# An expert loop's down projection: token rows straight out of the product, in place of a transposed result that is turned back

## The chip, the core and the metric

The kernel runs on one core of one Trainium2 chip. The metric is the device time of one execution in microseconds (us), lower is better. The core's engines work side by side, each through its own queue in order: TensorE (PE; its weight loads are listed apart as PEld), VectorE (DVE), ScalarE (ACT), GpSimd (POOL) and SyncE (SP), which here only starts transfers.

## The reference

An attention step gives 49,152 rows `x` of 128 numbers (4 batches of 12,288). Each row then goes through a mixture of 8 experts with one expert per row, and only if its skip score is positive:

```python
out = x.copy()
xc = x[x @ w_skip > 0]
probs = softmax(xc @ w_gate); e_idx = argmax; gate_w = probs of that expert
for e in range(8):
    h = np.maximum(xc[e_idx == e] @ w1[e], 0)          # 128 -> 1024
    y[e_idx == e] = gate_w[:, None] * (h @ w2[e])      # 1024 -> 128
out[x @ w_skip > 0] = xc + y
```

The change touches the last product, `h @ w2[e]`, and what follows it.

## The kernel before

**First part.** Attention runs in tiles of 128 queries. Each finished row is written to the output and, with its gate, its index and a scale, to a scratch table `scr` in which the rows of an expert lie together.

**Expert loop.** The second part works through groups of 2,048 rows of one expert, four blocks `s` of 512 tokens each. The first group is interleaved with the end of the attention (`peel`); the others run in a hardware loop whose body is the four blocks and whose count, 17 here, is read from a table at run time. A block is held transposed, channels on the partitions: `up` makes 8 chunks of 128 hidden channels x 512 tokens, `down` adds all chunks up to a result of 128 output channels x 512 tokens in one PSUM bank.

**Three products for one.** Weights and activations are split into two halves of 16 bits, `hi` and `lo`; each chunk costs the products hi·hi, lo·hi and hi·lo. So a block has 24 products in `up` and 24 in `down`, all of 512 columns. Each chunk of `up` fills one of four PSUM banks (pool `ps_h`); ACT takes `h_hi` out (relu, L294), then DVE takes `h_lo` out (L295), and only then is the bank free for the chunk four later.

**What follows `down` before the change.** ACT copies the bank to `yT` with the weights' scale `y_sc` (L310). In the next block, after the fourth chunk of `up`, `finish` has TensorE turn `yT` back in four transposes of 128 tokens (L315, bank pool `ps_x`); DVE works out the row indices (`ids`, L322) and adds gate times result to the input row (`o`, L326, one for each 128 tokens); POOL scatters the rows in four indirect transfers (L184). Then SP loads the next rows (`load_x`).

**Order.** The order on each engine is the order of the calls (`tc.manual_schedule()`); each engine runs its list in order and waits where it needs another's result. Besides the blocks' own work the loop prepares the next expert's weights: `split_w2` in block 0 (ACT makes `w2_hi`, L261, then DVE `w2_lo`, L263), `w_scale` spread over blocks 1 and 2 (DVE finds the largest weights, L207 to L216; a small TensorE product, L219, spreads them over the partitions; DVE reads it, L222, and makes the scales, L224 to L229), `split_w1` in block 3. `previous_stage_wait` marks where an engine makes sure of its block before; the loop's stages let no engine run two blocks ahead of another.

Of the kernel before, what the change touches and what calls it, by code (L numbers as in the profile page):

```python
# [9 lines left out]
F32 = mybir.dt.float32  # L10
# [5 lines left out]
ALU = mybir.AluOpType  # L16
AX = mybir.AxisListType
PSUM = bass.MemoryType.PSUM
# [6 lines left out]
def kernel(  # L25
# [11 lines left out]
    nc = tc.nc  # L37
# [117 lines left out]
    w2_hi = wp.tile([P, FC, C], F16, name="w2_hi")  # L155
    w2_lo = wp.tile([P, FC, C], F16, name="w2_lo")
    yTs = [wp.tile([P, ST], F32, name=f"yT{s}") for s in range(2)]
    xin = [wp.tile([P, TT, ROW], F32, name=f"xin{s}") for s in range(NST)]
    x16s = [wp.tile([P, 2, TT, C], F16, name=f"x16{i}") for i in range(2)]
    xT = [wp.tile([P, 2 * TT, P], F16, name=f"xT{s}") for s in range(NST)]  # L160
# [2 lines left out]
    def alloc_h(pool):  # L163
        h.update(hi=pool.tile([P, FC, ST], F16, name="h_hi"), lo=pool.tile([P, FC, ST], F16, name="h_lo"))
# [133 lines left out]
    def down(s):  # L298
# [10 lines left out]
                yield  # L309
        nc.scalar.activation(out=yTs[s % 2], in_=ps, func=AF.Copy, scale=y_sc[:, 0:1])  # L310

    def finish(s, g=None):
        ps = alloc["x"]()
        for t in range(TT):
            nc.tensor.transpose(ps[:, t * P:(t + 1) * P], yTs[s % 2][:, t * P:(t + 1) * P], ident)  # L315
        ids = xin[s].bitcast(I32)[:, :, C + 1:C + 2]
        own = op.tile([P, TT, 1], I32, name="ids")
        if g is None:
            nc.vector.tensor_copy(own, ids)
        else:  # L320

            nc.vector.scalar_tensor_tensor(out=own, in0=place[:, s, :].unsqueeze(2), scalar=low[:, bass.ds(g, 1)], in1=ids,  # L322
                                           op0=ALU.add, op1=ALU.max)
        o = op.tile([P, TT, C], F32, name="o")
        for t in range(TT):
            nc.vector.scalar_tensor_tensor(out=o[:, t, :], in0=ps[:, t * P:(t + 1) * P],  # L326
                                           scalar=xin[s][:, t, C:C + 1], in1=xin[s][:, t, 0:C],
                                           op0=ALU.mult, op1=ALU.add)

        def write():  # L330
            for t in range(TT):
                scatter_rows(out, own[:, t, :], o[:, t, :], NT - 1, "out")

        if g is None and not ready:
            held.append(write)
        else:
            write()

    def make_table():
        en = accs["run"]  # L340
# [48 lines left out]
    def peel(load_next):  # L389
        for s in range(NST):  # L390
            for c in range(FC):
                up(s, [c])
                if s > 0 and c == 3:
                    finish(s - 1)
                    load_next(s - 1)
                if s >= 2 and c == XP2:
                    x_transpose(s - 2)
                yield
            for _ in down(s):
                yield  # L400
            yield

    order = tc.manual_schedule()
    order.__enter__()
    with ExitStack() as p1:
        kprep = p1.enter_context(tc.tile_pool(name="kprep", bufs=1))
        kvm = p1.enter_context(tc.tile_pool(name="kvm", bufs=2))
# [607 lines left out]
        while t < NTILE + LAG - 1 or next_l or jobs:  # L1015
            t += 1
            b, tb = divmod(t, TPB)
            live = t < NTILE
            late_a.extend(next_l)
            next_l.clear()  # L1020
            if 0 <= t - TLAG < NTILE:
                p_transpose(t - TLAG)
            if live:
                scores(t, range(2) if t > 1 else [1])
            if 0 <= t - LAG < NTILE:
                attend(t - LAG)
            if live:
                row_max(t)
            if t in q_late:
                q_late.pop(t)()  # L1030
            if live and pools and next(pools[0], "end") == "end":
                pools.pop(0)
            run_late(early_a)
            run_late(split_a)
            if 0 <= t - 1 < NTILE:
                p_hi(t - 1)
            run_late(late_a)
            if live:
                row_exp(t)
            run_late(early_g)  # L1040
            run_late(split_v)
            run_late(early_v)
            if 0 <= t - 1 < NTILE:
                p_lo(t - 1)
            if live:
                if t % GT == 0:
                    if t > 0 and t // GT + QA < NGRP:
                        load_q(t // GT + QA)
                if b + 1 < B:
                    for k, r in KV_T.get(tb, ()):  # L1050
                        load_kv(b + 1, k, [r])
                if b + 1 < B and tb == PREP_T[0]:
                    work = prep_kv(b + 1)
                    preps += [(t + x - tb, work) for x in PREP_T]
                if t in PAD_T:
                    write_pads(PADS.pop(0))
            if t == NTILE - FIRST:
                assert not PADS and (SNAPR < 0 or first_writes)
                early.append(first_group())
            if early and live and next(early[0], "end") == "end":  # L1060
                early.pop(0)
            if t == NTILE:
                p_s.close()
                p_kv.close()
                p_q.close()
                alloc_h(p1.enter_context(tc.tile_pool(name="hp1", bufs=1)))
                ps_up = p1.enter_context(tc.tile_pool(name="ps_up", bufs=4, space=PSUM))
                alloc["h"] = lambda: ps_up.tile([P, ST], F32, name="up_ps")
            ph = t % GT
            if ph == 1 and t // GT + 2 < NGRP:  # L1070
                q_split(t // GT + 2, t)
            run_jobs(ph)
            if preps and preps[0][0] == t:
                next(preps.pop(0)[1], None)
            if live and b + 1 < B:
                for k, r in KV_T.get(tb - 4, ()):
                    if r == R - 1:
                        pools.append(pool_kv(b + 1, k))
            for _ in range(2 * (t >= NTILE)):
                next(first)  # L1080
# [5 lines left out]
        for _ in first:  # L1086
            pass
        n_it = nc.values_load(cumi[0:1, 0:1], min_val=1, max_val=NG + 1)
        idle = alloc["h"]()
        for _ in range(W4):  # L1090
            nc.tensor.matmul(idle, w1_hi[:, 0:P], h["hi"][:, 0, :], start=True, stop=True)

    with ExitStack() as p2:
        alloc_h(p2.enter_context(tc.tile_pool(name="hp", bufs=1)))
        ps_h = p2.enter_context(tc.tile_pool(name="ps_h", bufs=4, space=PSUM))
        ps_y = p2.enter_context(tc.tile_pool(name="ps_y", bufs=1, space=PSUM))
        ps_x = p2.enter_context(tc.tile_pool(name="ps_x", bufs=2, space=PSUM))

        alloc.update(h=lambda: ps_h.tile([P, ST], F32, name="h_ps"), x=lambda: ps_x.tile([P, ST], F32, name="x_ps"),
                     y=lambda: ps_y.tile([P, ST], F32, name="y_ps"))  # L1100
        alloc["w"] = alloc["x"]
        tc.prologue_barrier()
        order.__exit__(None, None, None)
        with tc.For_i(0, n_it, 1, hint_engines=(mybir.EngineType.PE,), iteration_sync="staggered") as i:
            for s in range(NST):
                prv = (s - 1) % NST
                with tc.manual_schedule():
                    up(s, range(0, 1))
                    for eng in (nc.gpsimd, nc.sync):
                        tc.previous_stage_wait(eng.engine)  # L1110
                    up(s, range(1, 3))
                    for eng in (nc.vector, nc.scalar, nc.tensor):
                        tc.previous_stage_wait(eng.engine)
                    up(s, range(3, 4))
                    if s == 0:
                        split_w2()
                    finish(prv, i if s == 0 else i + 1)
                    if s == 0:
                        load_w(i + 1)
                    load_x(load_start(i if s == 0 else i + 1), prv)  # L1120
                    up(s, range(4, FC))
                    x_transpose((s + 2) % NST)
                    if s == 1:
                        scale = w_scale()
                        next(scale)
                    if s in (1, 2):
                        next(scale, None)
                    if s == NST - 1:
                        split_w1()
                    for _ in down(s):  # L1130
                        pass
                if s < NST - 1:
                    tc.stage_boundary()
        finish(NST - 1, n_it)


_INS = ["q", "kv", "w_sr", "moe_w_skip", "moe_w_gate", "moe_w1", "moe_w2"]
# [35 lines left out]
```

## Time and profile before

| | |
|---|---|
| median of 3 runs | 1768.91 us (1766.88 to 1768.92) |
| the profiled execution, its own time | 1771.09 us |
| span of its trace | 1768.6 us |
| granted TensorE clock, mean of the span | 0.994 |
| loop, from its first product to its last | 1020 to 1759 us |

The trace's times count from the span's start. A line of the time line has start, duration, engine, source line, operation, what is written and read, the shapes and a count of merged instructions (the duration is then of all of them together); in square brackets stands how long the engine was idle before it and what released it. A TensorE product's duration holds the passage through the array, so products overlap: what one costs the engine is the distance between two starts.

### The profile page before, as it was taken

To read this page: it belongs to the slowest core of one execution; us is meant where nothing else is said; L and a number is where in the kernel's file an instruction comes from. 1 tells how busy PE (TensorE), PEld (TensorE's weight loads), DVE (VectorE), ACT (ScalarE), POOL (GpSimd) and SP (SyncE) were. 2 spreads that over 40 slices of the span, in tenths; PEclk is the share of its full clock that TensorE was granted. 3 is DMA by queue.
4 is the path that set the end of the run, shared out by engine and by line. 5 is a ranking of instruction groups with operands and counts; after the bars stand their busy time and mean duration, and the time that the engine had idled before them with its cause. 6 is when DMAs were issued, how large, how long until landed. Compare 5 with 4: busy or idle time off the path is not lost. (4 is left out here: it accounts for less than half of the span.)

```text
span 1768.6 us, 41455 instructions
## 1 busy us (share of the span) xinstructions
PE 1722.5 (97%) x13918; PEld 1242.3 (70%) x13918; DVE 1491.0 (84%) x3181; ACT 1314.3 (74%) x2487; POOL 631.0 (36%) x796
## 2 busy tenths in 40 slices
PE   5999999999999999999999899999999999999997
PEld 4999999999999998999898444444444444444443
DVE  7888899988998898999997778888877888888886
ACT  4888888888888888888897456666666666666664
POOL 3234333444334343323231323333333333333334
PEclk9999999999999999999999999999999999999999
DMA  7999999999999999999997333433333333333333
GB/s 222 213 200 237 230 198 213 225 233 222 211 224 229 222 191 232 205 188 210 218 210 157 98 79 99 102 99 98 99 101 99 97 97 99 103 101 98 100 105 79
DMA packets 608482, 284.81 MB, mean 161 GB/s; under 512 B 495440, under 2 KB 564176, under 8 KB 608336
## 3 DMA queue, kind: packets, MB, share of 16 engines
q1 hardware_dynamic: 586736, 222.76, 62.6%
q0 software_dynamic: 21600, 60.19, 13.1%
q8 instruction: 82, 1.34, 0.3%
q14 instruction: 64, 0.52, 0.1%
HBM read 90.47 MB, written 72.30 MB: 92 GB/s over the span
## 5 line engine op out<-in xcount | busy, mean ns | idle before, releaser
L295 DVE SCALAR_TENSOR_TENSOR h_lo<-h_ps,h_hi 128x512 f16<-128x512 f32 x544 | 343.8, 687 | 140.6 <-ACT h_hi L294 140.3
L184 POOL DMA_INDIRECT out_dram<-o,ids x288 | 283.1, 983 | 484.2 <-DVE o L326 415.4
L663 ACT ACTIVATE p_sb<-s_ps,nm 128x768 f32<-128x768 f32 x384 | 347.1, 904 | 117.0 <-DVE nm L658 113.1
L658 DVE TENSOR_REDUCE nm<-s_ps 128x1 f32<-128x768 f32 x384 | 365.4, 952 | 71.7 <-PE s_ps L652 68.6
L294 ACT ACTIVATE h_hi<-h_ps 128x512 f16<-128x512 f32 x544 | 316.9, 597 | 49.7 <-PE h_ps L293 30.8
L713 PE MATMUL acc_ps<-v_hi,pt 128*128 128x138 f16 x3072 | 320.0, 224 | 2.4 <-DMA pt<-p 2.3
L713 PEld LDWEIGHTS <-pt 128*128 128x128 f16 x4608 | 275.3, 97 | 64.1 <-issue 56.9
L713 PE MATMUL acc_ps<-v_lo,pt 128*128 128x138 f16 x1536 | 293.0, 223 | 0.0
L650 PE MATMUL s_ps<-k_hi,q_hi 128*128 128x384 f32 x768 | 291.8, 380 | 0.4 <-ACT k_hi L505 0.4
L671 DVE SCALAR_TENSOR_TENSOR p<-p_sb,p 128x512 f16<-128x512 f32 x384 | 270.3, 704 | 3.0 <-ACT p L667 1.6
L631 POOL TENSOR_TENSOR q_lo<-q_sb,q_hi 128x256 fp32r<-128x256 f32 (+1 forms) x190 | 146.8, 773 | 334.4 <-DVE p L671 198.4
L652 PE MATMUL s_ps<-k_hi,q_lo 128*128 128x384 f32 x768 | 259.1, 337 | 0.0
L651 PE MATMUL s_ps<-k_lo,q_hi 128*128 128x384 f32 x768 | 258.5, 337 | 0.0
L667 ACT ACTIVATE p<-p_sb 128x512 f16<-128x512 f32 x384 | 243.1, 633 | 5.5 <-DMA pt<-p 2.8
L291 PE MATMUL h_ps<-xT,w_hi 128*128 128x512 f16 x544 | 207.1, 381 | 6.5 <-issue 6.5
L310 ACT ACTIVATE yT<-y_ps,y_sc 128x512 f32<-128x512 f32 x68 | 46.7, 687 | 216.6 <-PE y_ps L307 213.2
L307 PEld LDWEIGHTS <-w_hi 128*128 128x128 f16 x1152 | 112.7, 98 | 134.8 <-issue 1.4
L292 PE MATMUL h_ps<-xT,w_hi 128*128 128x512 f16 x544 | 207.2, 381 | 0.0
L293 PE MATMUL h_ps<-xT,w_lo 128*128 128x512 f16 x544 | 207.2, 381 | 0.0
L307 PE MATMUL y_ps<-h_hi,w_hi 128*128 128x512 f16 x544 | 206.2, 379 | 0.0
L307 PE MATMUL y_ps<-h_hi,w_lo 128*128 128x512 f16 x544 | 206.2, 379 | 0.0
L307 PE MATMUL y_ps<-h_lo,w_hi 128*128 128x512 f16 x544 | 195.1, 379 | 0.0
(215 smaller groups left out, 2927.7 us busy)
## 6 DMA issues: line engine op xcount, KB each, us to landing
q_sb<-in_q_dram SPq DMA_DIRECT2D x96, 256.0 KB
out_dram<-rows SPq DMA_DIRECT2D x96, 256.0 KB
xin<-scr SPq DMA_DIRECT2D x75, 276.0 KB
w_raw<-in_moe_w_dram SPq DMA_DIRECT2D x34, 512.0 KB, 3.5
kvt<-in_kv_dram POOLq DMA_DIRECT2D x54, 256.0 KB
pt<-p SPq DMA_TRANSPOSE x384
kvt<-in_kv_dram SPq DMA_DIRECT2D x11, 512.0 KB
kvt<-in_kv_dram SPq DMA_DIRECT2D x20, 256.0 KB
```

Of the source, the lines that this page charges most:

```text
L184: ins = nc.gpsimd.indirect_dma_start(out=dst, out_offset=bass.IndirectOffsetOnAxis(ap=ids, axis=0), in_=src, in_offset=None, bounds_check= ...
L294: nc.scalar.activation(out=h["hi"][:, c, :], in_=ps, func=AF.Relu)
L295: nc.vector.scalar_tensor_tensor(out=h["lo"][:, c, :], in0=ps, scalar=0.0, in1=h["hi"][:, c, :], op0=ALU.max, op1=ALU.subtract)
L307: nc.tensor.matmul(ps, w[:, c, :], h[x][:, c, :], start=(i == 0), stop=(i == len(terms) - 1))
L650: nc.tensor.matmul(s[:, h, :HK], q_hi, k_hi[:, sl], start=True, stop=False)
L651: nc.tensor.matmul(s[:, h, :HK], q_hi, k_lo[:, sl], start=False, stop=False)
L652: nc.tensor.matmul(s[:, h, :HK], q_lo, k_hi[:, sl], start=False, stop=True)
L658: nc.vector.tensor_reduce(out=NM[t], in_=S_PS[t][:, :, :HK], axis=AX.XY, op=ALU.max, negate=True)
L663: nc.scalar.activation(out=P_SB[t], in_=S_PS.pop(t)[:, :, :HK], func=AF.Exp, bias=NM.pop(t))
L667: nc.scalar.activation(out=P16[t][:, 0, :], in_=p_flat(t)[:, 0:KD * P], func=AF.Copy, scale=2.0 ** PEXP)
L671: LO[:] = [nc.vector.scalar_tensor_tensor(out=p16[:, 1, :], in0=p_flat(t)[:, 0:KD * P], scalar=2.0 ** PEXP, in1=p16[:, 0, :], op0=ALU.mult ...
L713: nc.tensor.matmul(ps[:, j % 2, :], w, v[a][:, k, :], start=(i == 0), stop=(i == len(AVL) - 1))
```

## The change

In the loop, and for the last block of the first group, `down_rows` takes the place of `down`: the hidden values of 128 tokens are the stationary operand and `w2` (128 columns) streams past them, so the result has tokens on the partitions. That makes 96 products of 128 columns in a block, into four PSUM banks, one for each 128 tokens. `yT` and the transposes go; the gates are multiplied with `y_sc` by one small DVE instruction (`gy`), and the rows are taken out of the four banks as the first thing of the next block, ahead of its `up`; the scatter and the loads stay where they were. With four banks for the result, four are left for `up`; the small product of `w_scale` takes one of those too, and its step is moved behind block 2's `down_rows`. The first group's hidden tiles are kept for the loop, and `down_rows` of its last block stands behind the reading of the loop's count.

```diff
+    gy = wp.tile([P, TT, 1], F32, name="gy")
...
+    def down_rows(s):
+        ps = alloc["r"]
+        for c in range(FC + DL):
+            for t in range(TT):
+                sl = slice(t * P, (t + 1) * P)
+                if c < FC:
+                    for w in (w2_hi, w2_lo):
+                        nc.tensor.matmul(ps[t], h["hi"][:, c, sl], w[:, c, :], start=(c == 0 and w is w2_hi), stop=False)
+                if c >= DL:
+                    nc.tensor.matmul(ps[t], h["lo"][:, c - DL, sl], w2_hi[:, c - DL, :], start=False,
+                                     stop=(c == FC + DL - 1))
+
     def finish(s, g=None):
         ps = alloc["x"]()
         for t in range(TT):
             nc.tensor.transpose(ps[:, t * P:(t + 1) * P], yTs[s % 2][:, t * P:(t + 1) * P], ident)
+        send_out(s, [ps[:, t * P:(t + 1) * P] for t in range(TT)], xin[s][:, :, C:C + 1], g)()
+
+    def out_rows(s, g):
+        nc.vector.tensor_scalar(out=gy, in0=xin[s][:, :, C:C + 1], scalar1=y_sc[:, 0:1], scalar2=None, op0=ALU.mult)
+        return send_out(s, alloc["r"], gy, g)
+
+    def send_out(s, ps, gates, g):
...
-            nc.vector.scalar_tensor_tensor(out=o[:, t, :], in0=ps[:, t * P:(t + 1) * P],
-                                           scalar=xin[s][:, t, C:C + 1], in1=xin[s][:, t, 0:C],
-                                           op0=ALU.mult, op1=ALU.add)
+            nc.vector.scalar_tensor_tensor(out=o[:, t, :], in0=ps[t], scalar=gates[:, t, :],
+                                           in1=xin[s][:, t, 0:C], op0=ALU.mult, op1=ALU.add)
...
-            for _ in down(s):
-                yield
+            if s < NST - 1:
+                for _ in down(s):
+                    yield
...
+    with ExitStack() as p2:
+        ps_y = p2.enter_context(tc.tile_pool(name="ps_y", bufs=1, space=PSUM))
+        alloc["r"] = [ps_y.tile([P, ST], F32, name=f"y_ps{t}")[:, 0:C] for t in range(TT)]
+        down_rows(NST - 1)
         idle = alloc["h"]()
...
+        p_up.close()
         ps_h = p2.enter_context(tc.tile_pool(name="ps_h", bufs=4, space=PSUM))
-        ps_y = p2.enter_context(tc.tile_pool(name="ps_y", bufs=1, space=PSUM))
-        ps_x = p2.enter_context(tc.tile_pool(name="ps_x", bufs=2, space=PSUM))
...
+        alloc["h"] = lambda: ps_h.tile([P, ST], F32, name="h_ps")
+        alloc["w"] = alloc["h"]
...
                 with tc.manual_schedule():
+                    write = out_rows(prv, i if s == 0 else i + 1)
                     up(s, range(0, 1))
...
                     up(s, range(3, 4))
                     if s == 0:
                         split_w2()
-                    finish(prv, i if s == 0 else i + 1)
+                    write()
...
-                    if s in (1, 2):
+                    if s == 1:
                         next(scale, None)
                     if s == NST - 1:
                         split_w1()
-                    for _ in down(s):
-                        pass
+                    down_rows(s)
+                    if s == 2:
+                        next(scale, None)
...
-        finish(NST - 1, n_it)
+        out_rows(NST - 1, n_it)()
```

## Rows read from the trace of the kernel before

**Rows 1.** The page: busy time by engine; the costliest DVE group.

```profile
PE 1722.5 (97%) x13918; PEld 1242.3 (70%) x13918; DVE 1491.0 (84%) x3181; ACT 1314.3 (74%) x2487; POOL 631.0 (36%) x796
...
L295 DVE SCALAR_TENSOR_TENSOR h_lo<-h_ps,h_hi 128x512 f16<-128x512 f32 x544 | 343.8, 687 | 140.6 <-ACT h_hi L294 140.3
```

**Rows 2.** Windows: one pass of the loop, busy us (instructions) by engine, clock, DMA.

```profile
1498.91:1542.20 43.29, 43.29 (x210) 20.73 (x209) 35.19 (x82) 27.95 (x54) 15.72 (x16) 1.00 0.39 99
```

**Rows 3.** Time line of TensorE over that pass: where its stages begin.

```profile
1498.91 0.38 PE L291 MATMUL h_ps<-xT,w_hi 128*128 128x512 f16 x1
...
1501.50 0.60 PE L315 MATMUL x_ps<-ident,yT 128*128 128x128 f32 x4
1501.93 0.38 PE L291 MATMUL h_ps<-xT,w_hi 128*128 128x512 f16 x1
...
1504.52 0.38 PE L307 MATMUL y_ps<-h_hi,w_hi 128*128 128x512 f16 x1
...
1509.70 0.38 PE L291 MATMUL h_ps<-xT,w_hi 128*128 128x512 f16 x1
...
1531.41 0.38 PE L291 MATMUL h_ps<-xT,w_hi 128*128 128x512 f16 x1
...
1542.20 0.38 PE L291 MATMUL h_ps<-xT,w_hi 128*128 128x512 f16 x1
```

**Rows 4.** Time line of TensorE in the attention: products of 138 columns.

```profile
600.45 0.22 PE L713 MATMUL acc_ps<-v_lo,pt 128*128 128x138 f16 x1
...
601.35 0.22 PE L713 MATMUL acc_ps<-v_lo,ptq 128*128 128x138 f16 x1
```

**Rows 5.** Time line of TensorE: two products of the routing, 8 and 1 columns.

```profile
986.48 0.17 PE L812 MATMUL acc_ps<-inner,ones_bf 128*128 128x8 bf16 x1
986.51 0.16 PE L813 MATMUL acc_ps<-odd,ones_bf 128*128 128x1 bf16 x1
```

**Rows 6.** Time line of DVE over the same pass of the loop.

```profile
1500.62 2.49 DVE L295 SCALAR_TENSOR_TENSOR h_lo<-h_ps,h_hi 128x512 f16<-128x512 f32 x4 [2.47 <-ACT h_hi L294]
1503.36 1.28 DVE L263 SCALAR_TENSOR_TENSOR w_lo<-w_raw,w_sc,w_hi 128x1024 f16<-128x1024 f32 x1 [0.26 <-ACT w_hi L261]
...
1518.49 2.34 DVE L207 TENSOR_REDUCE w_max<-w_raw 128x1 f32<-128x1024 f32 x2
...
1521.07 0.48 DVE L216 TENSOR_SCALAR w_dg<-ident,w_max 128x128 bf16<-128x128 f32 x2
...
1524.66 0.22 DVE L322 SCALAR_TENSOR_TENSOR ids<-place,low,xin 128x4 int32<-128x4 f32 x1
1524.79 1.12 DVE L326 SCALAR_TENSOR_TENSOR o<-x_ps,xin 128x128 f32<-128x128 f32 x4
1525.82 2.48 DVE L295 SCALAR_TENSOR_TENSOR h_lo<-h_ps,h_hi 128x512 f16<-128x512 f32 x4
...
1529.26 0.42 DVE L222 TENSOR_REDUCE w_max<-x_ps 128x2 f32<-128x256 f32 x1
...
1530.25 0.20 DVE L229 TENSOR_SCALAR y_sc<-w_exp 128x1 f32<-128x1 f32 x1
```

**Rows 7.** Time line of the weight loads: the second of block 0's down projection.

```profile
1504.70 0.10 PEld L307 LDWEIGHTS <-w_lo 128*128 128x128 f16 x1 [0.29 <-DVE w_lo L263]
```

**Rows 8.** Time line where the loop begins.

```profile
1018.08 0.69 ACT L310 ACTIVATE yT<-acc_ps,y_sc 128x512 f32<-128x512 f32 x1 [11.98 <-remote]
...
1020.13 0.58 PE L291 MATMUL h_ps<-xT,w_hi 128*128 128x512 f16 x1 [6.54 <-issue]
```

**Rows 9.** The page: transfers of instructions, count, MB and share.

```profile
q8 instruction: 82, 1.34, 0.3%
```

**Rows 10.** Time line of the end: last products, first rows, first scatter.

```profile
1758.25 0.59 PE L307 MATMUL y_ps<-h_lo,w_hi 128*128 128x512 f16 x2
...
1760.32 0.87 DVE L326 SCALAR_TENSOR_TENSOR o<-x_ps,xin 128x128 f32<-128x128 f32 x3 [0.33 <-PE x_ps L315]
...
1760.94 0.98 POOL L184 DMA_INDIRECT out_dram<-o,ids  x1 [3.31 <-DVE o L326]
```

More of the change, by code (lines that the diff above doesn't have):

```diff
@@ L332, in write @@
                 scatter_rows(out, own[:, t, :], o[:, t, :], NT - 1, "out")
[L334 to L337, printed above, removed]
+        return (lambda: held.append(write)) if g is None and not ready else write
     def make_table():
@@ L404 @@
     order.__enter__()
+    p_up = ctx.enter_context(ExitStack())
     with ExitStack() as p1:
@@ L1065 @@
                 p_q.close()
-                alloc_h(p1.enter_context(tc.tile_pool(name="hp1", bufs=1)))
-                ps_up = p1.enter_context(tc.tile_pool(name="ps_up", bufs=4, space=PSUM))
+                alloc_h(ctx.enter_context(tc.tile_pool(name="hp", bufs=1, side="right")))
+                ps_up = p_up.enter_context(tc.tile_pool(name="ps_up", bufs=4, space=PSUM, side="right"))
                 alloc["h"] = lambda: ps_up.tile([P, ST], F32, name="up_ps")
@@ L1091 @@
             nc.tensor.matmul(idle, w1_hi[:, 0:P], h["hi"][:, 0, :], start=True, stop=True)
-    with ExitStack() as p2:
-        alloc_h(p2.enter_context(tc.tile_pool(name="hp", bufs=1)))
+        p_up.close()
         ps_h = p2.enter_context(tc.tile_pool(name="ps_h", bufs=4, space=PSUM))
-        ps_y = p2.enter_context(tc.tile_pool(name="ps_y", bufs=1, space=PSUM))
-        ps_x = p2.enter_context(tc.tile_pool(name="ps_x", bufs=2, space=PSUM))
-        alloc.update(h=lambda: ps_h.tile([P, ST], F32, name="h_ps"), x=lambda: ps_x.tile([P, ST], F32, name="x_ps"),
-                     y=lambda: ps_y.tile([P, ST], F32, name="y_ps"))
-        alloc["w"] = alloc["x"]
+        alloc["h"] = lambda: ps_h.tile([P, ST], F32, name="h_ps")
+        alloc["w"] = alloc["h"]
         tc.prologue_barrier()
```

## The prediction, made before the changed kernel was run

> **What bounds the kernel now.** I read the page first: TensorE is busy for 97% of the span, DVE for 84% [rows 1]. The change lies in the expert loop, so the windows of one pass of the loop come next: TensorE is busy for all of its 43.29 us at full clock, DVE for 35.19 [rows 2]. Then the time line of TensorE through that pass. Twelve products of 512 columns take 2.59 us (1501.93 to 1504.52), 0.2158 each; a block's 48 take 10.36. The four transposes hold TensorE for 0.43 (1501.50 to 1501.93). Blocks 1 and 2 together last 21.71, which is 0.13 more than two such blocks: the small product of `w_scale`. Four blocks and that are 43.29 [rows 3]: nothing is left over, TensorE never waits in the loop. Anything taken from it is a gain, and any new wait on it is a loss, at once. The page's 544 `h_lo` [rows 1] are 32 for each pass, so there are 17 passes, and 0.1 us in a pass is 1.7 us.
>
> DVE has room, but not everywhere. Before the first `h_lo` of a block it stands idle (2.47 us in block 0), and that first `h_lo` starts 1.71 us after the block's first product (1500.62 against 1498.91) [rows 3, 6]; I use 1.65 for the other blocks, whose ACT work is the same. Four `h_lo` take 2.48 together and one 0.687 [rows 1, 6], so they follow each other every 0.60, a little faster than the chunks (3 x 0.2158 = 0.647).
>
> **TensorE's own work.** No row has 128 columns of 16 bits at full clock, but its neighbours stand on both sides. Fifteen products of 138 columns, each with a weight load of its own as everywhere in this program (as many loads as products [rows 1]), take 0.90 us, 60.0 ns each [rows 4]; 512 columns take 215.8 [rows 3]. The line through both gives 55.8 ns at 128. The load is no floor there: two products that hardly stream anything follow each other in 30 ns at most, loads included [rows 5]. Bounds: 55.7 (60.0 in proportion to the columns) and 60.0 (not slower than the longer one). I take 55.8, since both neighbours lie on one line with a plausible fixed part of 2 to 3 ns. Then 96 products take 5.36 us, where 24 took 5.18: +0.18. The transposes go: -0.43. A block gains 0.25 and a pass 1.0. With 60.0 it would lose 0.6 in a pass instead.
>
> [...]
>
> **Block 0: `w2_lo` is late.** DVE makes `w2_lo` after ACT's `w2_hi`, which is itself behind the fourth relu; it ends at 1503.36 + 1.28 = 1504.64, 5.73 us after the block's first product, and the weight load that waited for it went 0.06 later [rows 3, 6, 7]. Before, the transposes pushed the down projection back and a first product of 0.22 stood ahead, so the wait was just covered. Now `up` ends at 5.18 and the second product, 0.06 later, already streams `w2_lo`. ACT's and DVE's chain up to there is unchanged: it hangs on the fourth chunk, ahead of the old transposes. TensorE waits from 5.23 to 5.79: 0.56 us. Bounds: 0.30, if the 0.26 that DVE waited for ACT goes away, and 1.6, if the rows taken out first push all of DVE back by their 1.17.
>
> **Taking rows out first.** `gy` is new; its nearest row is `ids`, 0.22 long and 0.13 ahead of the next start. `gy`, `ids` and four `o` (1.03 from the first to what follows) [rows 6] stand ahead of the first `h_lo`. The `o` can start some 0.2 after the block before has ended, when its last products have passed the array, and end by about 1.3, before `h_lo` is due at 1.65: they cost nothing as long as the idle time there covers them. If it were gone, up to 1.4 a block. In block 1 DVE is fullest: the `w_scale` steps end 3.06 after their first reduction starts (1518.49 to 1521.55) [rows 6]. After the change the `h_lo` end 6.85 into the block, four `x` splits follow (about 1.05, as the `o`), so the steps run from 7.8 to 10.9; block 2 starts at 10.5. `gy` begins 0.4 late, the first `h_lo` is at about 1.6 of block 2, on time by a hair. I take nothing, 0.3 as the upper bound.
>
> **Block 3: the scale step now stands in the way.** This is the main loss. The small product follows block 2's last one. DVE waits for it (its reduction can start about 0.28 into block 3, counting 0.27 for the product's passage, less the 0.12 that it keeps TensorE, and 0.1 of handing over), then needs 0.99 to the start of the last scale, some 0.15 more to `gy`, 0.13 to `ids`, 0.13 to the first `o` and 1.03 through the four [rows 6]. The first `h_lo` starts at 2.7 in place of 1.65, ends at 3.4, and its bank is free at about 3.47. With four banks, one of them lent to the scale product but given back early, the fifth chunk must wait for that bank, and it is due after four chunks, at 2.59. TensorE stands for 0.88 us; afterwards the `h_lo` keep ahead (0.60 against 0.647). Bounds: 0.3, if the small steps overlap nearly wholly, and 1.3, with slower handings-over.
>
> **What moves without a cost.** ACT loses `yT`. POOL's scatters and SP's loads of the next rows keep their place in the queues but find their rows earlier; both end well inside the block, and behind them wait only the next block's. The last block's down projection of the first group moves behind the loop's count; TensorE is idle for 6.54 us before the loop starts [rows 8], which covers it; uncovered it would be 5.4.
>
> **End.** TensorE's last product is issued by 1758.68 (two from 1758.25) and the first scatter starts at 1760.94, 2.26 later, with `yT` and the transposes between [rows 10]. Now `o` starts at about 0.1 and the scatter 0.62 behind it, as in these rows: 1.5 us gained.
>
> **Sum.** A pass: -1.0 + 0.56 + 0.88 = +0.44; 17 passes +7.5; the end -1.5: +6.0. The profiled execution took 1771.1 in all (span 1768.6 and 2.5 around it), so it would take 1777.1. The median of the runs, 1768.9, is 2.2 below it: 1774.9, slower by 0.34%. A measurement of this kernel can tell about 0.2%, 3.5 us, from no change.
>
> **Rivals.**
> *The gain stays* (other side). The place is the fifth chunk of block 3. If its bank comes free with a wait of only 0.3, a pass changes by -0.14 and the kernel by 17 x -0.14 - 1.5 = -3.9: 1765. The point where it decides: below a wait of 0.53 the kernel is not slower, below 0.32 measurably faster. With both waits absent it would be 17 x -1.0 - 1.5 = -18.5: 1750. For it: DVE is idle for 8 us of a pass [rows 2]. Against: the idle time lies in front of the relus, and this chain hangs on the last product of the block before.
>
> *TensorE's instructions are fetched anew in each pass.* The program's 13,918 products and as many loads [rows 1], less the repeats of 16 passes (418 each), are some 21,100 instructions in 82 transfers [rows 9], about 258 in each. A pass now has some 960, nearly four transfers' worth, where it had less than two. If the core doesn't keep that many, the jump back waits. The trace bounds the price: entering the loop, TensorE began 2.05 after ACT went on [rows 8]; 17 times that is 35: 1810. For it: the queue of short products drains faster than before. Against: the attention streams instructions at this rate without a gap.
> [...]
>
> *The products cost more than the line says.* At 60 ns each a pass changes by +1.6 more: 1802. Against it stand the two neighbours on one line [rows 3, 4]. [...]
>
> *DVE is late in blocks 1 and 2 too*, by 0.3 each: 1785.
>
> **How the numbers follow.** My forecast 0.58 (of it 0.40 slower, 0.18 within 0.2%); gain stays 0.20 (0.17 faster, 0.03 within); fetched anew 0.07; dearer products 0.06; DVE late twice 0.09. Together faster 0.17, same 0.21, slower 0.62. The forecast's own range is 1770 to 1780 (0.15 us of each wait, 17 times, both ways). For 8 in 10 I leave out the upper rivals beyond 1790 and half of the gains: 1761 to 1790.
>
> **What would show it.** Starts of the down products every 56 ns; block 0's second one released by `w_lo` at about 5.8; in block 3 a hole of 0.9 before the fifth chunk, released by `h_lo`; no hole elsewhere; a pass of 43.7. It is wrong if those holes are missing, or a gap stands where the loop jumps back, or the products are further apart.

## The result and the profile after

The changed kernel took 1774.89 us (median; 1774.15 to 1790.61), where the kernel before took 1767.64 (1765.92 to 1768.92): a ratio of 1.0052, 95% interval 1.0034 to 1.007. It is slower, by 7.25 us or half a per cent. Forecast were 1774.9 and slower.

The profiled execution was the slowest of its runs (1790.61, span 1788.2). Its first part ended some 9 us later than that of the kernel before, which a second profile of it does not repeat; so its loop and its end are read here, and what lies ahead of the loop further down, from that second one. The page, TensorE and the other engines' busy lines and the transfers of instructions, beside [rows 1, 9]:

```profile
PE 1713.7 (96%) x18610; PEld 1423.6 (80%) x18610; DVE 1514.6 (85%) x3250; ACT 1268.7 (71%) x2418; POOL 632.0 (35%) x796
...
q8 instruction: 84, 1.38, 0.3%
```

TensorE is busy for less, but no longer all of the time. Windows of one pass of the loop and of its four blocks, then of blocks 1 and 2 of the next pass (busy us and instructions of PE, PEld, DVE, ACT, POOL; clock; DMA), beside [rows 2]:

```profile
1471.40:1515.02 43.62, 42.59 (x485) 30.95 (x483) 36.45 (x86) 25.33 (x50) 15.72 (x16) 1.00 0.37 98
1471.40:1482.53 11.13, 10.70 (x123) 7.75 (x121) 8.77 (x20) 6.49 (x13) 3.93 (x4) 1.00 0.53 153
1482.53:1493.07 10.54, 10.54 (x123) 7.71 (x121) 10.03 (x21) 5.94 (x12) 3.93 (x4) 1.00 0.38 91
1493.07:1503.72 10.65, 10.65 (x124) 7.79 (x122) 7.83 (x20) 5.94 (x12) 3.93 (x4) 1.00 0.30 76
1503.72:1515.02 11.30, 10.71 (x124) 7.70 (x121) 9.83 (x27) 6.96 (x13) 3.93 (x4) 1.00 0.29 71
1526.15:1536.69 10.54, 10.54 (x123) 7.71 (x121) 9.16 (x18) 5.94 (x12) 3.93 (x4) 1.00 0.30 75
1536.69:1548.06 11.37, 10.81 (x124) 7.80 (x122) 8.48 (x22) 5.94 (x12) 3.93 (x4) 1.00 0.36 86
```

A block without a wait takes 10.54; block 2 has the scale product on top (0.11). Blocks 0 and 3 are longer by 0.59 and 0.76. So the pass takes 43.62, 0.33 more than before; a pass without its two holes would take 42.27. In the next pass block 2 is late too (11.37), of which more below.

TensorE's time line in that pass shows the holes, the stretches in which it starts nothing (an "idle before" is counted from the modelled end of the product ahead, 0.38 or 0.22 long, and so is shorter by 0.16 than the hole between starts), beside [rows 3]:

```profile
1476.58 0.22 PE L320 MATMUL y_ps<-w_hi,h_hi 128*128 128x128 f16 x1
1477.23 0.22 PE L320 MATMUL y_ps<-w_lo,h_hi 128*128 128x128 f16 x1 [0.43 <-issue]
...
1503.72 0.38 PE L292 MATMUL h_ps<-xT,w_hi 128*128 128x512 f16 x1
...
1507.07 0.38 PE L292 MATMUL h_ps<-xT,w_hi 128*128 128x512 f16 x1 [0.59 <-DVE h_lo L296]
...
1509.66 0.22 PE L320 MATMUL y_ps<-w_hi,h_hi 128*128 128x128 f16 x1
...
1515.02 0.38 PE L292 MATMUL h_ps<-xT,w_hi 128*128 128x512 f16 x1
```

And DVE's, beside [rows 6]: `w_lo` of block 0, then the begin of block 3.

```profile
1475.86 1.32 DVE L264 SCALAR_TENSOR_TENSOR w_lo<-w_raw,w_sc,w_hi 128x1024 f16<-128x1024 f32 x1 [0.34 <-ACT w_hi L262]
...
1503.92 0.42 DVE L223 TENSOR_REDUCE w_max<-h_ps 128x2 f32<-128x256 f32 x1 [3.02 <-PE h_ps L220]
...
1504.91 0.20 DVE L230 TENSOR_SCALAR y_sc<-w_exp 128x1 f32<-128x1 f32 x1
1505.03 0.22 DVE L332 TENSOR_SCALAR gy<-xin,y_sc 128x4 f32<-128x4 f32 x1
1505.16 0.22 DVE L341 SCALAR_TENSOR_TENSOR ids<-place,low,xin 128x4 int32<-128x4 f32 x1
1505.30 1.12 DVE L345 SCALAR_TENSOR_TENSOR o<-y_ps,gy,xin 128x128 f32<-128x128 f32 x4
1506.33 1.88 DVE L296 SCALAR_TENSOR_TENSOR h_lo<-h_ps,h_hi 128x512 f16<-128x512 f32 x3
```

Block 0: `w_lo` ends at 1477.18 and the second down product, the first that needs it, begins at 1477.23, 0.65 behind the first where 0.06 is the step. The trace names no releaser there ("issue"); that it is `w_lo` follows from the end of DVE's row, 0.05 ahead, and from the third experiment. Block 3: five steps of the scale, `gy`, `ids` and four `o` stand in a row without a gap, and the first `h_lo` starts 2.61 us into the block. The fifth chunk was due at 2.59 and goes at 3.35, 0.05 after that `h_lo` has ended (1506.33 and 0.69 [rows 1]). Block 3's down projection takes 5.36 us from its first product (1509.66) to the next block (1515.02), so its 96 products are 55.8 ns apart.

The end, beside [rows 10]: TensorE's last products, the last rows, the first scatter.

```profile
1779.28 0.44 PE L322 MATMUL y_ps<-w_hi,h_lo 128*128 128x128 f16 x5
...
1779.92 1.12 DVE L345 SCALAR_TENSOR_TENSOR o<-y_ps,gy,xin 128x128 f32<-128x128 f32 x4
...
1780.54 0.98 POOL L185 DMA_INDIRECT out_dram<-o,ids  x1 [5.23 <-DVE o L345]
```

Five steps of 55.8 ns from 1779.28 end at 1779.56, and the scatter starts 0.98 later; counted in the same way it was 2.26 before.

### The profile page after: what moved, and what is told of

It is laid out like the page before. It is cut to its first block, busy times and chain, and to the rows that moved or that the text cites. A ratio compares the mean times of both kernels' runs of the same rounds, so it can differ in the third digit from the quotient of the medians.

```text
span 1788.2 us, 50409 instructions
## 1 busy us (share of the span) xinstructions
PE 1713.7 (96%) x18610; PEld 1423.6 (80%) x18610; DVE 1514.6 (85%) x3250; ACT 1268.7 (71%) x2418; POOL 632.0 (35%) x796
## 5 line engine op out<-in xcount | busy, mean ns | idle before, releaser
L320 PE MATMUL y_ps<-w_lo,h_hi 128*128 128x128 f16 x2208 | 361.2, 220 | 9.2 <-issue 8.8
L320 PE MATMUL y_ps<-w_hi,h_hi 128*128 128x128 f16 x2208 | 363.0, 220 | 5.2 <-issue 5.2
L320 PEld LDWEIGHTS <-h_hi 128*128 128x128 f16 x4416 | 333.6, 98 | 33.6 <-issue 17.6
L322 PE MATMUL y_ps<-w_hi,h_lo 128*128 128x128 f16 x2208 | 345.4, 220 | 0.5 <-issue 0.5
L688 DVE SCALAR_TENSOR_TENSOR p<-p_sb,p 128x512 f16<-128x512 f32 x384 | 274.1, 714 | 7.6 <-ACT p L684 6.1
L322 PEld LDWEIGHTS <-h_lo 128*128 128x128 f16 x2208 | 205.5, 98 | 0.7 <-issue 0.6
```

What stands on the lines that cost most here:

```text
L320: nc.tensor.matmul(ps[t], h["hi"][:, c, sl], w[:, c, :], start=(c == 0 and w is w2_hi), stop=False)
L322: nc.tensor.matmul(ps[t], h["lo"][:, c - DL, sl], w2_hi[:, c - DL, :], start=False, stop=(c == FC + DL - 1))
L688: LO[:] = [nc.vector.scalar_tensor_tensor(out=p16[:, 1, :], in0=p_flat(t)[:, 0:KD * P], scalar=2.0 ** PEXP, in1=p16[:, 0, :], op0=ALU.mult ...
```

## The experiments

Eleven runs, in three groups, each on one chip and beside runs of the kernel before: 1760.86 there for the first four, 1760.37 for the next four, 1768.18 for the last three.

**The changed kernel again** (`e1_after_again`), for a profile of a usual execution.

> The changed kernel as it is, once more, for a second profile. In its first profile, one of the slowest executions of it (1790.6 us against a median of 1774.9), a pass of the loop takes 43.62 us, 0.33 more than before; the attention part ends some 9 us later than before; and where the loop begins TensorE stands for 4 us over a few products without a wait that the profile names. I expect the same 43.62 a pass, with waits of 0.60 in block 0 and 0.75 in block 3, and a median of 1774 to 1776. If the 9 and the 4 us belong to that execution, they are gone here, and the profiled execution is at 1775 to 1779; if they belong to the change, they are here again.

1766.13 us, 1.0034 times the kernel before [1.0022, 1.0046]. The span is 1764.7, and its passes are 43.58 to 43.62 long; no block 2 is late. So in the loop it is two holes, 1.35 in a pass, that turn the gain of 1.02 into a loss of 0.33.

**The scale's last step early** (`e2_scale_early`): it stands ahead of block 2's down projection again, so its DVE steps run during that projection and not behind it.

```diff
-                    if s == 1:
+                    if s in (1, 2):
                         next(scale, None)
...
                     down_rows(s)
-                    if s == 2:
-                        next(scale, None)
```

> The last step of w_scale goes back ahead of block 2's down projection; all else as changed. My theory (block 3 waits because the reading of the small product and six small instructions stand between block 2's end and the rows that are taken out): the hole before block 3's fifth chunk goes, a pass falls by 0.75 us to 42.87, the kernel by 12.7 to 1762. Rival (DVE is too full, so a wait taken away here turns up as another): the pass stays above 43.4 and the kernel above 1771.

1751.25, 0.9947 [0.9934, 0.9961]; 14.9 below the changed kernel. Block 3's hole is gone: the pass below takes 42.92 and its block 3 10.60 (every second pass takes 42.82).

```profile
1440.64:1483.56 42.92, 42.48 (x485) 30.98 (x483) 36.84 (x87) 25.34 (x50) 15.74 (x16) 1.00 0.39 100
1472.96:1483.56 10.60, 10.60 (x124) 7.74 (x122) 8.95 (x20) 6.96 (x13) 3.93 (x4) 1.00 0.32 76
```

In the two profiles the loop from its first product to its last is 12.6 shorter (728.8 for 741.4), and it starts 2.7 earlier (1011.92 for 1014.66). Most of these 2.7 lies ahead of anything that the edit touches; what it comes from stays open.

**`w2_lo` needed later** (`e3_wlo_later`): its products come two chunks behind those of `w2_hi`.

```diff
-        for c in range(FC + DL):
+        LL = 2
+        for c in range(FC + LL):
...
-                    for w in (w2_hi, w2_lo):
-                        nc.tensor.matmul(ps[t], h["hi"][:, c, sl], w[:, c, :], start=(c == 0 and w is w2_hi), stop=False)
+                    nc.tensor.matmul(ps[t], h["hi"][:, c, sl], w2_hi[:, c, :], start=(c == 0), stop=False)
...
+                if c >= LL:
+                    nc.tensor.matmul(ps[t], h["hi"][:, c - LL, sl], w2_lo[:, c - LL, :], start=False,
+                                     stop=(c == FC + LL - 1))
```

> Only the order of the 96 products changes: those with w2_lo run two chunks behind those with w2_hi, so that 12 products (0.67 us) stand ahead of the first that needs w2_lo. My theory (block 0 waits 0.60 for w2_lo since nothing stands ahead of it any more): the hole goes, a pass falls by 0.60 to 43.02, the kernel by 10 to 1765. Rival (the wait is one for the jump or for the block before, and moves): still 43.6 a pass, 1775.

1756.4, 0.9972 [0.9961, 0.9984]; 9.7 below the changed kernel, 17 times 0.59 being 10.0. Every block 0 is at 10.54, block 3 still at 11.29 to 11.36.

```profile
1449.29:1459.83 10.54, 10.54 (x123) 7.71 (x121) 8.71 (x20) 6.49 (x13) 3.93 (x4) 1.00 0.52 151
1481.02:1492.38 11.36, 10.77 (x123) 7.72 (x121) 9.86 (x28) 6.96 (x13) 3.93 (x4) 1.00 0.30 71
```

**Both edits** (`e4_both`).

> Both edits together. My theory: the two waits are independent, TensorE has no hole left in the loop, a pass is its work alone, 4 x 10.54 + 0.11 = 42.27 us; the kernel is at 1775 - 17 x 1.35 = 1752, some 16 us faster than the kernel before. Rival (short products with a weight load each cost more than their spacing shows, or DVE becomes the bound): a pass stays above 43, the kernel above 1765.

1742.72, 0.99 [0.9885, 0.9916]: 23.4 below the changed kernel and 18.1 below the kernel before. The rival under which the gain stays had priced the state without either wait at -18.5. Windows of a pass: TensorE is busy in all of it, and so in every pass but the first (42.37).

```profile
1435.55:1477.82 42.27, 42.27 (x484) 30.93 (x482) 36.80 (x86) 25.33 (x50) 15.72 (x16) 1.00 0.38 101
```

**The kernel before again** (`e5_before_again`), for a second profile of where the loop begins.

> The kernel before, for a second profile. In the changed kernel's second profile the loop begins 15.6 us after the first group's fifth chunk of its last block (18.6 before, in the one profile of it) and starts at full clock, where before the first block took 13.3 us instead of 10.8. Passes (+0.33 each) and the end (-1.2) account for about +4 of the measured +5.3, so I expect that an ordinary execution of the kernel before begins its loop some 15 us after that point and without the cold first block, and that the 18.6 and 13.3 belong to the one execution. If they come back, the change gains about 5 us at the entry and something else must lose them.

1760.79, 1.0001 [0.999, 1.0012]. TensorE's time line, beside [rows 8]: the fifth chunk of `up` in the first group's last block, which serves as a mark here; the filler products, whose results nobody uses (L1091); the loop's first product. The stretch from the mark to the loop is called the entry.

```profile
999.40 0.38 PE L291 MATMUL up_ps<-xT,w_hi 128*128 128x512 f16 x1 [1.24 <-DVE h_lo L295]
...
1010.39 1.02 PE L1091 MATMUL up_ps<-h_hi,w_hi 128*128 128x512 f16 x4 [0.42 <-issue]
1012.21 0.38 PE L291 MATMUL h_ps<-xT,w_hi 128*128 128x512 f16 x1 [0.79 <-PE up_ps L1091]
```

TensorE is idle for 0.79 ahead of the loop, not for 6.54. The cover that I had counted on belonged to the first profile's execution. Nor did it cover anything in the first profile of the changed kernel, where the entry takes 22.15 (1010.68 to 1032.83, with slow stretches that the last section shows) for 18.61 (1001.52 to 1020.13). The same place in the changed kernel (the profile of the first experiment), TensorE's time line:

```profile
999.11 0.38 PE L292 MATMUL up_ps<-xT,w_hi 128*128 128x512 f16 x1 [1.27 <-DVE h_lo L296]
...
1006.53 0.22 PE L320 MATMUL y_ps<-w_hi,h_hi 128*128 128x128 f16 x1 [1.93 <-DVE h_lo L296]
...
1014.66 0.38 PE L292 MATMUL h_ps<-xT,w_hi 128*128 128x512 f16 x1
```

and DVE's:

```profile
1004.51 0.17 DVE L339 COPY ids<-xin 128x4 int32<-128x4 int32 x1 [2.42 <-DMA out_dram<-o,ids]
1004.59 1.12 DVE L345 SCALAR_TENSOR_TENSOR o<-acc_ps,xin 128x128 f32<-128x128 f32 x4
```

From the fifth chunk to the loop it is 12.81 before and 15.55 after: 2.74 more. The down projection that moved there waits 1.93 for an `h_lo` (3.41 to 3.49 for DVE in the second, third, fourth and sixth experiment). DVE does that `h_lo` right behind the rows of the block before, and it can't begin these rows until a scatter of an earlier block lands and gives back an `ids` buffer (2.42). DVE waits for a landing there in the kernel before too (2.52 in both its profiles), but the old projection could begin at once (0.21 behind the product ahead of it, in both). By the program the new one needs four banks that the first part used until then; that it is a bank it waits for is argued from that, and no row says it.

**Block 3's rows late** (`e6_rows_late_in_3`): the changed kernel, but in block 3 alone the rows are taken out behind the fourth chunk, as they were before. The scale's step stays late.

```diff
-                    write = out_rows(prv, i if s == 0 else i + 1)
+                    if s < 3:
+                        write = out_rows(prv, i if s == 0 else i + 1)
...
+                    if s == 3:
+                        write = out_rows(prv, i + 1)
```

> As changed, with the scale step behind block 2's down projection, but in block 3 alone the rows are taken out behind the fourth chunk, where the old finish stood. My theory (the hole in block 3 is the sum of a chain: small product, its reading, six small instructions, gy, ids and four o, all ahead of the first h_lo): without the last 1.3 us of the chain the first h_lo is due anyway at 1.65, the hole of 0.59 goes, a pass takes 42.87, some 1753 us here. Rival (the place of the small product alone makes the hole, by its bank or its wait): the hole stays, 1766.

1753.76, 0.9953 [0.9938, 0.9969]. DVE's time line of a block 3 that began at 1477.09:

```profile
1477.29 0.42 DVE L223 TENSOR_REDUCE w_max<-h_ps 128x2 f32<-128x256 f32 x1 [3.02 <-PE h_ps L220]
...
1478.28 0.20 DVE L230 TENSOR_SCALAR y_sc<-w_exp 128x1 f32<-128x1 f32 x1
1478.65 2.65 DVE L296 SCALAR_TENSOR_TENSOR h_lo<-h_ps,h_hi 128x512 f16<-128x512 f32 x4 [0.17 <-ACT h_hi L295]
1481.21 0.22 DVE L332 TENSOR_SCALAR gy<-xin,y_sc 128x4 f32<-128x4 f32 x1
```

The scale's steps begin as late as ever, but the first `h_lo` now follows them at 1.56 and the block takes 10.59. Neither the late small product nor the early rows make the hole alone; it is the two in one chain ahead of the first `h_lo`.

**Both edits, each `o` done twice** (`e8_both_rows_twice`), to find how much DVE work ahead of the `h_lo` is covered. The second `o` writes the same values again.

```diff
-            nc.vector.scalar_tensor_tensor(out=o[:, t, :], in0=ps[t], scalar=gates[:, t, :],
-                                           in1=xin[s][:, t, 0:C], op0=ALU.mult, op1=ALU.add)
+            for _ in range(2):
+                nc.vector.scalar_tensor_tensor(out=o[:, t, :], in0=ps[t], scalar=gates[:, t, :],
+                                               in1=xin[s][:, t, 0:C], op0=ALU.mult, op1=ALU.add)
```

> As with both edits, each of the four o of a block done twice (the same result). It asks how much idle time covers them. My theory (the o fill a hole that ends when the first h_lo is due at 1.65, and TensorE waits once the fifth chunk's bank is late): 1.04 us more on DVE pushes the first h_lo to about 2.35, 0.5 of waiting in three blocks and 0.8 in block 2: 2.3 a pass, 39 us, 1782. If DVE had room to spare everywhere: 1743. If all of it lay on the path: 71 us, 1814.

1806.29, 1.026 [1.0238, 1.0282], 24 above what I expected; a pass takes 45.8 in place of 42.27, and 17 times 3.5 are 60. TensorE's and DVE's time lines at a block 0 that began at 1427.95:

```profile
1427.98 2.67 DVE L348 SCALAR_TENSOR_TENSOR o<-y_ps,gy,xin 128x128 f32<-128x128 f32 x8 [0.72 <-PE y_ps L324]
1430.57 1.88 DVE L296 SCALAR_TENSOR_TENSOR h_lo<-h_ps,h_hi 128x512 f16<-128x512 f32 x3
...
1431.30 0.38 PE L292 MATMUL h_ps<-xT,w_hi 128*128 128x512 f16 x1 [0.60 <-DVE h_lo L296]
```

Eight `o` hold DVE for 2.59 up to the next start, four for 1.03: the second of a pair costs 0.39 and not 0.26. So the first `h_lo` starts at 2.62, and again the fifth chunk is 0.76 late. Three places agree (block 3 of the changed kernel, the late block 2 shown further down, this block): 2.58 to 2.62 us to the first `h_lo` give 0.72 to 0.76 of hole. Block 2 of this run lies on the same line, 3.10 to the `h_lo` and a hole of 1.24 (11.89 for 10.65). So there should be no hole up to some 1.86. Blocks 2 of other passes show it: a first `h_lo` at 1.85 makes no hole and one at 1.90 makes 0.04 (both in the ninth experiment's profile), one at 1.88 makes 0.02 (the changed kernel's first profile). The `h_lo` of an undisturbed block starts at about 1.57: it may come 0.3 us late at no cost, and what comes later is paid in full.

**A third buffer for `ids` and `o`** (`op` with `bufs=3` in place of 2), to take the landing out of the loop's entry: with both edits (`e7_both_op3`, and again as `e11_both_op3_again` beside `e10_both_again`, the kernel with both edits alone), and in the changed kernel (`e9_after_op3`).

```diff
-    op = ctx.enter_context(tc.tile_pool(name="op", bufs=2))
+    op = ctx.enter_context(tc.tile_pool(name="op", bufs=3))
```

> As with both edits, and a third buffer for the row indices and the rows that go out. At the entry of the loop TensorE stands 3.4 us ahead of down_rows until an h_lo behind the rows of the block before, and DVE had stood 2.4 us for the landing of a scatter to get a buffer for the indices. If that buffer is what holds the entry, the wait shrinks by 2.4 us and the kernel to 1740.5. If the entry hangs on the scatters themselves or on the reading of the count, 1743 as without.

> The changed kernel with three buffers in place of two for ids and o, and nothing else. Theory (the changed kernel pays some 2.7 us where it enters the loop, because the first group's last down projection needs a bank that rows still stand in, and those rows stand 2.4 for the landing of a scatter that frees an ids buffer): the wait for the landing goes, the loop starts some 12 behind the first group's last fifth chunk in place of 15.5, and the kernel ends some 2.5 earlier, 1763.6 where the changed kernel takes 1766.1. Rival (what is won there is given back in the first block of the loop, whose weights or rows are not there earlier): the loop starts earlier, its first block lasts longer by as much, and the time stays 1766.

> The kernel with both edits (scale step early, w2_lo two chunks later) again, beside the next one on the same chip: 1742 to 1743, first part of the usual length, 15.5 from the first group's last fifth chunk to the loop, no hole in the loop.

> The same with three buffers for ids and o, beside the one before on the same chip. Theory (the entry is on the path): 4.2 won at the entry less 0.5 in the first block, so 3.7 less than the one before, about 1739. Rival (given back before the loop, the first part being longer with three buffers): equal to it within 1 us, and the first part some us longer in this profile too.

No gain came in any of them. The first: 1742.45, 0.9891 [0.9875, 0.9908], no less than both edits alone; this is the 1743 of its second reading and not the 1740.5 of the theory. The other three missed on both readings: 12 above the rival's 1766, 10 above 1743, and 3.7 above the run beside it, where 3.7 below or the same was expected. The changed kernel with it: 1778.38, 1.005 [1.0033, 1.0067], against ratios of 1.0052 and 1.0034 without, on other chips. On that chip both edits alone took 1753.06, 0.9911 [0.9895, 0.9928], and with the buffer 1756.75, 0.9927 [0.9911, 0.9943]. In the first one's time line (`e7_both_op3`) the wait at the entry falls from 3.45 to 0.86, and the loop starts 11.25 behind the fifth chunk where both edits alone needed 15.45 (the wait makes 2.6 of it; the other 1.6 is the projection, 5.36 at a granted clock of 1.00 in place of 6.94 at 0.76):

```profile
1011.89 0.44 PE L320 MATMUL y_ps<-w_hi,h_hi 128*128 128x128 f16 x5 [0.86 <-DVE h_lo L296]
```

But in all three profiles with three buffers that fifth chunk comes later, at 1007.09, 1005.04 and 1005.28; with both edits alone it comes at 997.32 and 996.59, in the other profiles with two buffers at 996.86 to 1003.26, but for the first one's 1010.68. The program also has 49 more instructions (50,475 against 50,426, both edits in each), so more than a buffer differs in the first part. And two of the three profiled executions with three buffers (`e7_both_op3`, `e9_after_op3`) were the slowest of their runs, 5.7 above the median, so part of the lateness may be theirs: this is no clean test of the entry. That DVE waits for a landing there is shown, and in the one pair of profiles from the quicker chips (the fourth and the seventh) the wait goes with the buffer; what the entry would be worth by itself stays open.

## Why the prediction was right, and where it was not

**Sum.** It was predicted at +6.0 and 1774.9; measured are +7.25 and 1774.89, and on another chip +5.3. Between the profiles of the first and fifth experiments, both ordinary executions on chips with the same time before: first part -0.3 (999.11 against 999.40), entry +2.74, seventeen passes of +0.33 make +5.6, end -1.28, together +6.8; the spans differ by 6.6 (1764.7, 1758.1). The first part is the loosest of these: its mark lies between 996.59 and 1003.26 in the changed kernels with two buffers, the first profile aside. So the mechanism in the loop was right, and that the time came out to 0.01 is luck. Two errors cancel in part, a pass that was priced 0.11 too dear (+0.44 for +0.33, 1.9 us in 17) and an entry priced at nothing (+2.7); and the kernel before measured 1767.64 beside the changed one, 1.3 below the 1768.91 that the forecast was added to.

**TensorE's own work.** Right. Products are 55.8 ns apart, as predicted; a block without waits 10.54, and 42.27 a pass against 43.29, a gain of 1.02 for the 1.0 predicted. The rival of dearer products, at 60 ns, has fallen: 96 pairs of load and product in a row kept 55.8 at a granted clock of 1.00.

**Block 0.** Right: `w_lo` ends 5.78 into the block (5.73 predicted), and the block is 0.59 longer (0.56 predicted). The third experiment takes just this away. The upper bound of 1.6 does not come out of its own terms (0.56 and 1.17 are 1.73); nothing rests on it.

**Block 3.** Right in place and mechanism, its term 0.12 too large: 0.76 for 0.88. DVE's first step begins 0.20 into the block and not at 0.28. The parts named for the 0.28 add up to 0.25 only, and the handing over took 0.04 of the 0.1 put on it: the small product keeps TensorE 0.11 and lasts 0.27. From there on the chain takes 2.41, where the steps from [rows 6] add up to 2.43. The second and the sixth experiment break the chain in two ways, and either removes the hole. This wait is above 0.53, where the forecast said that the sign turns, so "the gain stays" did not come; the fourth experiment shows what that rival's kernel without both waits is worth: -18.1 for the -18.5 that it gave. There too terms make up for each other: against the fifth experiment's profile, the loop gains 17.2 and the end 1.3, about as priced, the entry loses 2.6, and a first part that happened to end 2.1 earlier gives most of that back.

**Block 2, "on time by a hair".** Right in an ordinary execution: `gy` starts 0.18 into the block (1493.25), the `h_lo` at 1.57. But the hair broke in 7 of the 17 passes of the first profile, and in 7, 6 and 3 of the last group's three profiles; in the first experiment's in none. ACT's, DVE's and TensorE's rows where it does:

```profile
1532.64 0.60 ACT L295 ACTIVATE h_hi<-h_ps 128x512 f16<-128x512 f32 x1 [0.83 <-PE y_ps L320]
...
1533.28 0.69 DVE L296 SCALAR_TENSOR_TENSOR h_lo<-h_ps,h_hi 128x512 f16<-128x512 f32 x1 [0.74 <-ACT h_hi L295]
...
1537.90 0.22 DVE L332 TENSOR_SCALAR gy<-xin,y_sc 128x4 f32<-128x4 f32 x1
...
1539.27 3.07 DVE L296 SCALAR_TENSOR_TENSOR h_lo<-h_ps,h_hi 128x512 f16<-128x512 f32 x5
...
1540.00 0.38 PE L292 MATMUL h_ps<-xT,w_hi 128*128 128x512 f16 x1 [0.56 <-DVE h_lo L296]
```

The last relu of block 1 starts after 0.83 of idle time, 6.49 into its block where 5.47 is usual. Everything behind it on DVE shifts, `gy` comes 1.21 into block 2 for the usual 0.18, and the block lasts 0.72 longer. So the rival "DVE late in blocks 1 and 2" has half come true, in one block, in some passes, at more than the 0.3 of my bound: 7 times 0.7 is 5 us, which an ordinary execution on the other chips does not pay. What holds the relu back, the trace does not name (the product ahead had long been issued); it stays open.

**The entry.** This is the step that failed: "TensorE is idle for 6.54 us before the loop starts [rows 8], which covers it". The prediction took the 6.54 us of idle time in front of the loop as cover for the down projection that moved there, from one profile. A second profile of the same kernel has 0.79 there. The gap was not even free time in the first: the block behind it took 13.32 at a mean granted clock of 0.81 (0.56 up to 1026.00), where that of the second profile, behind 0.79, took 10.79 at 1.00. Nor was it the projection's 5.4 us that was paid in full: it takes the place of 24 products of 5.18 [rows 3] that stood ahead of the loop already, and what is new is a wait ahead of it, for an `h_lo` behind rows that themselves wait for a landing (1.93 of idle time in the first experiment's profile), and a lower clock. Windows of the projection, the first experiment's and then the fifth's:

```profile
1006.53:1013.51 6.98, 6.98 (x96) 6.95 (x96) 2.62 (x7) 0.00 (x0) 5.38 (x6) 0.76 0.53 126
...
1003.18:1010.39 7.21, 5.78 (x25) 2.34 (x24) 4.64 (x13) 1.07 (x3) 5.38 (x7) 1.00 0.45 111
```

Between these two profiles the 2.74 divide so: the chunks from the mark on take 5.11 at a clock of 0.67 for 3.57 at 1.00 (+1.5); the projection begins 2.31 after the last of them for 0.21 (+2.1); it takes 6.98 for 7.21, which held 1.0 of idle time (-0.2); the loop follows 1.15 after its end for 1.82 (-0.7). The prediction had the entry at nothing. Why the clock falls in one and not in the other stays open.

**The end.** -1.28 (2.26 to 0.98 between the two ordinary profiles) for -1.5.

**Instructions fetched anew.** Fallen: there are 84 transfers of instructions for 82 before [rows 9], and no gap where the loop jumps back (43.62 from jump to jump, every part of it accounted for). Across the jump the last five products, from 1514.74 on, and the next pass's first, at 1515.02, are 56 ns apart, in a pass of 485 products and 483 loads.

## What to carry to other kernels

Before taking work off the engine that bounds the loop, list what that work was covering: here four transposes, 0.43 us in all, hid `w2_lo`, and rows taken out behind the fourth chunk left DVE free ahead of the first `h_lo`; both came back as waits, of 0.59 and 0.76. What makes the change pay is to move two things: the scale's last step ahead of block 2's down projection, and the products that need `w2_lo` two chunks back (0.99 of the time before instead of 1.0034, on one chip). An idle stretch that is to cover something should be seen in more than one profile.

## What was unexpected of the hardware

In the eighth experiment a DVE operation that writes the same output again starts 0.39 behind the one ahead of it, one on the next tile 0.27. DVE's time line:

```profile
1428.37 0.35 DVE L348 SCALAR_TENSOR_TENSOR o<-y_ps,gy,xin 128x128 f32<-128x128 f32 x1
...
1428.64 0.34 DVE L348 SCALAR_TENSOR_TENSOR o<-y_ps,gy,xin 128x128 f32<-128x128 f32 x1
```

The first `o` starts at 1427.98 and lasts 0.35. Its repeat starts 0.39 after it, when it has ended; the `o` of the next tile starts 0.27 after that, before the repeat has ended. The lines name no releaser there, so whether the repeat waits by the program or by the engine itself is not shown.

On the chip of the last three runs, where the kernel before took 1768, the loop's entry has stretches in which TensorE gets on by one instruction, load or product, every 0.71 us, with no wait that the trace names. TensorE's and its weight loads' time line in the ninth experiment:

```profile
1014.22 0.22 PE L320 MATMUL y_ps<-w_hi,h_hi 128*128 128x128 f16 x1 [1.24 <-issue]
...
1014.93 0.10 PEld L320 LDWEIGHTS <-h_hi 128*128 128x128 f16 x1 [1.35 <-issue]
1015.65 0.22 PE L320 MATMUL y_ps<-w_lo,h_hi 128*128 128x128 f16 x1 [1.21 <-issue]
...
1016.36 0.10 PEld L322 LDWEIGHTS <-h_lo 128*128 128x128 f16 x1 [1.33 <-issue]
1017.07 0.22 PE L322 MATMUL y_ps<-w_hi,h_lo 128*128 128x128 f16 x1 [1.21 <-issue]
```

There the entry takes 21.54 to 21.78 us, with two buffers and with three; on the other two chips 11.25 to 16.63 in all eight profiles, none of which has such stretches. The first profile of the changed kernel has one, and its entry takes 22.15. The cause stays open.
